# Fourier feature stage of a delta-rule attention and MLP kernel: cosine and sine sums kept apart for half of the outputs

## The chip, the cores and the metric

The kernel runs on one core of a Trainium2 chip. The metric is the device time of one execution in microseconds; lower is better. A core has five engines that run side by side, each with a queue of its own: PE (TensorE, matrix products; its weight loads are listed as PEld), DVE (VectorE), ACT (ScalarE), POOL (GpSimd) and SP, which here only issues DMAs. PE reads its operands from SBUF and writes to PSUM, from where DVE and ACT take the results.

## The reference

Three stages follow one another, on 4 batches of 768 positions and 384 features, all in fp32:

```python
# 1: delta-rule attention, 8 heads of 48; a state of 48x48 per head is carried over the positions
# 2: Fourier mixing and a feed-forward block
X = np.fft.fft(x, axis=1)
X = np.fft.fft(X, axis=2)
u = x + np.real(X)
un = (u - mean(u)) / sqrt(var(u) + 1e-6)
x2 = u + np.maximum(un @ w_ch1, 0.0) @ w_ch2
# 3: token mixing with cos and sin of x2 @ w_theta, then a second small feed-forward
```

The change lies in the second Fourier transform of stage 2, the one over the 384 features.

## The kernel before

Attention is worked off in chunks of 64 positions. When the 12 chunks of a batch are done, `fourier_inputs` forms sums and differences of that batch's rows and folds the features: because the cosine is even and the sine odd, feature d and feature 384-d are added for the cosine sums and subtracted for the sine sums, which leaves 384 folded rows instead of two times 384. `fourier_1` multiplies these by the position table `cs1` and leaves `G`, three chunks of 128 folded features by 385 position columns. Chunks 0, 1 and 2 of `G` hold the cosine rows 0 to 191, then 191 sine rows, and the cosine row 192 last.

Stage 2 works in 12 blocks, three per batch, of 256 positions each: position t and its mirror 768-t side by side (`u[:, 0]` and `u[:, 1]`). `prepare_1` multiplies `G` by the feature table `cs2` to get `pm`, 128 positions by 385 features. The mirrored positions need no product of their own: their feature e is feature 384-e of `pm`, read backwards. Only in the last block of a batch (`j == 2`) one row (position 384) is its own, and it has the small product `px`. Then come the adds to the residual `u`, the mean and the variance (`bn_stats`), and the normalised `un`. `prepare_2` transposes `un` on PE and splits it into a high and a low part. Twelve steps `f` follow per block: `ffn_up` gives `ph` (9 matmuls), ACT makes `hh` and DVE `hl` of it, and `ffn_down` adds six products into `pc`.

The order around the change is written out by hand: with `LEAD = (0, 4, 11)` the three parts of the next block's preparation (`prepare`, `prepare_1`, `prepare_2`) are issued at steps f = 0, 4 and 11 of the block before. So the adds of a block stand on DVE's queue between the `hl` evictions (L586) of the running block. Attention of the later batches is issued between the steps as filler. The compiler's planner then sets the final order on each engine from a simulated timeline. `pm`, `px`, `pg`, `ph` and `pt` share one PSUM pool of three buffers (tag `g`).

An fp32 matmul in the source shows as two matmul instructions in the trace, each streaming all its columns.

Of the kernel before, what the change touches and what calls it, by code (L numbers as in the profile page):

```python
# [10 lines left out]
F32 = mybir.dt.float32  # L11
# [8 lines left out]
DM = H * D  # L20
# [116 lines left out]
class Front:  # L137
# [60 lines left out]
    def mm(self, o, l, r):  # L198
        self.nc.tensor.matmul(o, l, r, start=True, stop=True, skip_group_check=True)  # L199

    def gram(self, w, c0=0, c1=2 * C):

# [183 lines left out]
    def fourier_inputs(self, b):  # L386

        nc = self.nc
        y = [self.y.pop((b, k)) for k in range(NT)]
        HD = DM // 2  # L390
        SQ = math.sqrt(3.0) / 2.0
        alone = b < FDVE

        def tt(o, a, c, op, dve=False):
            (nc.vector if dve or alone else nc.gpsimd).tensor_tensor(o, a, c, op)

        def new(nm):
# [12 lines left out]
        tt(y4, y4, y3, ALU.subtract)  # L410
        nc.scalar.activation(y4, y4, AF.Copy, scale=SQ)
        nc.vector.scalar_tensor_tensor(y3, y5, -0.5, t0, ALU.mult, ALU.add)
        tt(t0, t0, y5, ALU.add)
        tt(y5, y1, y2, ALU.subtract, True)
        tt(y1, y1, y2, ALU.add)
        nc.scalar.activation(y1, y1, AF.Copy, scale=-SQ)
        nc.vector.scalar_tensor_tensor(y2, y5, 0.5, y0, ALU.mult, ALU.add)
        tt(y0, y0, y5, ALU.subtract, True)

        def fold(o, d0, n, z, op, flip=False, dve=False):  # L420
            a = z[:, d0:d0 + n]
            r = z[:, DM - d0:DM - d0 - n:-1]
            if flip:
                a, r = r, a
            tt(o, a, r, op, dve)

        out = {}
        for r, zc, zn, p1, p2 in ((1, y2, y1, y5, t1), (2, y3, y4, y2, y1)):
            fold(p1[:, 0:HD], 0, HD, zc, ALU.add, dve=True)
            fold(p1[:, HD:DM - 1], 1, HD - 1, zn, ALU.subtract, dve=True)  # L430
            nc.scalar.activation(p1[:, DM - 1:DM], zc[:, HD:HD + 1], AF.Copy)
            fold(p2[:, 0:HD], 0, HD, zn, ALU.add)
            fold(p2[:, HD:DM - 1], 1, HD - 1, zc, ALU.subtract, flip=True)
            nc.scalar.activation(p2[:, DM - 1:DM], zn[:, HD:HD + 1], AF.Copy)
            out[f"p1{r}"], out[f"p2{r}"] = p1, p2
        for r, z, p in ((3, y0, y3), (0, t0, y4)):
            fold(p[:, 0:HD], 0, HD, z, ALU.add, dve=True)
            fold(p[:, HD:DM], 1, HD, z, ALU.subtract, flip=True)
            e = self.fz.tile([P, 32], F32, tag=f"e{r}", name=f"e{r}_{b}")
            nc.gpsimd.memset(e[:, 0:31], 0.0)  # L440
            nc.scalar.activation(e[:, 31:32], z[:, HD:HD + 1], AF.Copy)
            out[f"q{r}"], out[f"e{r}"] = p, e
        self.z[b] = out

    def fourier_1(self, b):
# [13 lines left out]
        for ch in range(KD):  # L459
# [19 lines left out]

    def residual(self, u, b, i):  # L480
# [43 lines left out]
    def prepare_1(self, b, j, u, un):  # L524
        nc, cs2, G = self.nc, self.cs2, self.G[b]
        HD = DM // 2
        k = f"{b}_{j}"
        pm = self.psg.tile([P, DM + 1], F32, tag="g", name=f"pm{k}")
        for ch in range(KD):
            nc.tensor.matmul(pm, G[:, ch, j * P:(j + 1) * P], cs2[:, ch, :], start=(ch == 0), stop=(ch == KD - 1))  # L530
        if j == 2:
            px = self.psg.tile([P, DM + 1], F32, tag="g", name=f"px{k}")
            for ch in range(KD):
                nc.tensor.matmul(px[64:65, 0:HD + 1], G[:, ch, DM:DM + 1], cs2[:, ch, 0:HD + 1], start=(ch == 0),
                                 stop=(ch == KD - 1))
        nc.vector.tensor_tensor(u[:, 0, :], u[:, 0, :], pm[:, 0:DM], ALU.add)
        v = u[:, 1, :]
        if j < 2:
            nc.vector.tensor_tensor(v, v, pm[:, DM:0:-1], ALU.add)
# [433 lines left out]
def constants():  # L973
# [55 lines left out]
```

## Time and profile before

| | |
|---|---|
| time, median of 3 runs (lowest, highest) | 1001.06 us (999.76, 1001.69) |
| span of the profiled execution (no other time is recorded for it) | 1217.0 us |
| mean granted clock of PE in it | 0.666 of full speed |
| PE busy (PEld) | 1126.0 us, 93% (957.3 us) |
| DVE, ACT, POOL busy | 682.7, 394.8, 387.5 us |

The profiled execution is 216 us longer than the median of the timed runs. All durations below are from it. "Busy" of PE counts the time in which any matmul is under way, and ends of matmuls are modelled.

### The profile page before, as it was taken

The numbers are of one execution on the slowest core, as the hardware profiler recorded it, in microseconds if no ns is written. First come the engines' busy times: TensorE is split into PE (matmuls) and PEld (weight loads), VectorE is DVE, ScalarE is ACT, GpSimd is POOL, SyncE is SP. The second block draws the span as 40 slices with busy tenths as digits, with TensorE's granted clock in tenths as the row PEclk, the third lists the DMA queues.
The fourth block names the chain that finished last, engine by engine and source line by source line (L and its number), as shares of the span: only waits on it lengthen the run. The fifth ranks groups of instructions, "written<-read, shape, count | busy, mean of one in ns | idle before, by whom it ended". The sixth has DMA issues, their size and how long they took to land.

```text
span 1217.0 us, 23437 instructions
## 1 busy us (share of the span) xinstructions
PE 1126.0 (93%) x9312; PEld 957.3 (79%) x9312; DVE 682.7 (56%) x1574; ACT 394.8 (32%) x982; POOL 387.5 (32%) x504
## 2 busy tenths in 40 slices
PE   5675664999999999999999999999999999999998
PEld 4564553778788888788888898888988888888887
DVE  5999999645666632576212464744579732450401
ACT  2243343423332343244352121212545411460300
POOL 5257764341131113024120242430235421350210
PEclk9995555666666666666666666666666666666666
DMA  6223431221030021012030021311132201110000
GB/s 190 70 87 94 121 110 50 79 72 60 29 110 21 28 86 59 27 40 68 27 106 14 26 78 40 91 40 32 47 104 65 85 14 35 38 40 20 20 13 26
DMA packets 42206, 71.87 MB, mean 59 GB/s; under 512 B 6833, under 2 KB 27057, under 8 KB 42097
## 3 DMA queue, kind: packets, MB, share of 16 engines
q1 hardware_dynamic: 41328, 68.02, 18.7%
q0 software_dynamic: 768, 2.36, 0.7%
q8 instruction: 73, 1.20, 0.4%
q14 instruction: 37, 0.30, 0.1%
HBM read 56.20 MB, written 14.16 MB: 58 GB/s over the span
## 4 chain that ended last, share of the span: by engine, by line
PE 83%; DVE 13%; issue 1%; DMA 1%; ACT 1%; POOL 0%; SPq 0%; ACTq 0%; DVEq 0%; POOLq 0%
PE pc L595 6%; PE ph L72 6%; PE ph L74 6%; PE ph L73 6%; PE pc L598 6%; PE pc L596 6%; PE ty L73 6%; PE ty L72 6%; PE ty L74 6%; PE sm L199 3%; PE pm L530 3%; DVE tmp L258 3%; DVE T L261 3%; PE py L199 2%; PE pg L457 2%; PE pu L199 2%
## 5 line engine op out<-in xcount | busy, mean ns | idle before, releaser
L586 DVE SCALAR_TENSOR_TENSOR hl<-ph,hh 128x256 fp32r<-128x256 f32 x144 | 60.1, 421 | 196.6 <-ACT hh L585 164.1
L72 PE MATMUL ph<-uh,w1h 128*128 128x256 f32 x432 | 151.9, 355 | 0.0
L74 PE MATMUL ph<-uh,w1l 128*128 128x256 f32 x432 | 148.5, 345 | 0.0
L73 PE MATMUL ph<-ul,w1h 128*128 128x256 f32 x432 | 148.2, 344 | 0.0
L595 PE MATMUL pc<-w2h,hh 128*128 128x384 f32 x288 | 127.6, 443 | 0.0
L585 ACT ACTIVATE hh<-ph 128x256 fp32r<-128x256 f32 x144 | 54.5, 383 | 208.6 <-PE ph L74 183.0
L596 PE MATMUL pc<-w2l,hh 128*128 128x384 f32 x288 | 121.4, 422 | 0.0
L199 PE MATMUL sm<-kt 48*64 48x128 f32 (+1 forms) x896 | 87.5, 354 | 30.7 <-DMA kt<-in_kq_dram 17.3
L73 PEld LDWEIGHTS ph<-ul,w1h 128*128 128x128 f32 x432 | 100.7, 233 | 6.6 <-issue 2.2
L72 PEld LDWEIGHTS ph<-uh,w1h 128*128 128x128 f32 x432 | 97.4, 226 | 8.3 <-issue 2.5
L74 PEld LDWEIGHTS ph<-uh,w1l 128*128 128x128 f32 x432 | 101.0, 234 | 2.3 <-issue 0.8
L199 PEld LDWEIGHTS sm<-kt 48*64 48x64 f32 x896 | 67.5, 186 | 43.7 <-ACT KQ L220 12.5
L598 PE MATMUL pc<-w2h,hl 128*128 128x384 f32 x288 | 98.2, 425 | 0.0
L261 DVE TENSOR_TENSOR T<-T,tmp 128x30 f32<-128x30 f32 (+9 forms) x180 | 73.1, 406 | 4.2
L258 DVE TENSOR_TENSOR tmp<-T 128x30 f32<-128x30 f32 (+9 forms) x180 | 72.9, 405 | 4.3
L284 POOL TENSOR_SCALAR_AFFINE_SELECT YQ<-KQ 64x512 f32<-64x512 f32 x48 | 33.1, 690 | 131.5 <-PE py L199 122.8
L199 PE MATMUL py<-X,YQ 112*64 112x48 f32 (+1 forms) x768 | 54.4, 259 | 22.3 <-ACT X L340 22.1
L595 PEld LDWEIGHTS pc<-w2h,hh 128*128 128x128 f32 x288 | 63.3, 220 | 8.4 <-issue 4.0
L596 PEld LDWEIGHTS pc<-w2l,hh 128*128 128x128 f32 x288 | 63.2, 220 | 7.2 <-issue 1.7
L199 PE MATMUL pu<-X,YU 128*64 128x48 f32 (+1 forms) x768 | 46.2, 262 | 23.6 <-ACT X L352 11.7
L199 PEld LDWEIGHTS py<-X,YQ 112*64 112x64 f32 (+1 forms) x768 | 45.3, 184 | 28.7 <-ACT X L340 23.9
L199 PEld LDWEIGHTS pu<-X,YU 128*64 128x64 f32 (+1 forms) x768 | 38.7, 181 | 33.9 <-ACT X L352 12.2
(282 smaller groups left out, 2524.6 us busy)
## 6 DMA issues: line engine op xcount, KB each, us to landing
kt<-in_kq_dram SPq DMA_DIRECT2D x96, 96.0 KB, 2.2
w_0raw<-in_w_dram SPq DMA_DIRECT2D x15, 384.0 KB, 3.4
YQ<-in_qt_dram SPq DMA_DIRECT2D x48, 96.0 KB, 2.4
Y<-in_kn_dram SPq DMA_DIRECT2D x48, 96.0 KB, 2.4
X<-in_v_dram SPq DMA_DIRECT2D x48, 96.0 KB, 2.5
ysc<-y SPq DMA_DIRECT2D x24, 192.0 KB, 2.1
x2scr<-u SPq DMA_DIRECT2D x12, 384.0 KB, 2.8
xt<-x2scr SPq DMA_DIRECT2D x24, 192.0 KB, 2.4
```

The lines of the kernel that those rows point to most:

```text
L72: nc.tensor.matmul(out, lh, rh, start=start, stop=False)
L73: nc.tensor.matmul(out, lh, rl, start=False, stop=False)
L74: nc.tensor.matmul(out, ll, rh, start=False, stop=stop)
L199: self.nc.tensor.matmul(o, l, r, start=True, stop=True, skip_group_check=True)
L258: nc.vector.tensor_tensor(pr, T[:, j + 1:, j:j + 1].to_broadcast([P, n, j]), T[:, j, 0:j].unsqueeze(1).to_broadcast([P, n, j]), ALU.mult)
L261: nc.vector.tensor_tensor(T[:, j + 1:, 0:j], T[:, j + 1:, 0:j], pr, ALU.add)
L530: nc.tensor.matmul(pm, G[:, ch, j * P:(j + 1) * P], cs2[:, ch, :], start=(ch == 0), stop=(ch == KD - 1))
L585: nc.scalar.activation(hh, ph, AF.Relu)
L586: self.up_end = nc.vector.scalar_tensor_tensor(hl, ph, 0.0, hh, ALU.max, ALU.subtract)
L595: nc.tensor.matmul(self.pc[i], hh[:, i * P:(i + 1) * P], wh, start=(f == 0), stop=False)
L596: nc.tensor.matmul(self.pc[i], hh[:, i * P:(i + 1) * P], wl, start=False, stop=False)
L598: nc.tensor.matmul(self.pc[i], hl[:, i * P:(i + 1) * P], wh, start=False, stop=(f == KF - 1))
```

## The change

`cs2` is cut from 385 output columns to 193, and kept apart for cosine and sine: four pieces of 128 rows by 193 columns instead of three of 128 by 385. The feature order is moved so that the 193 cosine rows come first and the 191 sine rows last. Chunk 0 of `G` is then all cosine, chunk 2 all sine, chunk 1 mixed. `pm` becomes two halves, cosine sums (`pm[:, 0]`) and sine sums (`pm[:, 1]`), 193 columns each. Feature e is their sum, feature 384-e their difference. ACT copies the cosine half to a new tile `c`, DVE forms the sum `lo` and the difference `hi` in `un`, and four adds of 193 or 191 columns bring them to the two halves of `u`, in place of two adds of 384 columns read from PSUM.

```diff
     def mm(self, o, l, r, start=True, stop=True):
...
-        self.cs2 = p.tile([P, KD, DM + 1], F32, name="cs2")
+        self.cs2 = p.tile([P, 4, DM // 2 + 1], F32, name="cs2")
...
+            fold(p1[:, HD + 1:DM], 1, HD - 1, zn, ALU.subtract, dve=True)
+            nc.scalar.activation(p1[:, HD:HD + 1], zc[:, HD:HD + 1], AF.Copy)
...
-            fold(p[:, HD:DM], 1, HD, z, ALU.subtract, flip=True)
+            nc.gpsimd.memset(p[:, HD:HD + 1], 0.0)
+            fold(p[:, HD + 1:DM], 1, HD - 1, z, ALU.subtract, flip=True)
             e = self.fz.tile([P, 32], F32, tag=f"e{r}", name=f"e{r}_{b}")
-            nc.gpsimd.memset(e[:, 0:31], 0.0)
-            nc.scalar.activation(e[:, 31:32], z[:, HD:HD + 1], AF.Copy)
+            nc.gpsimd.memset(e[:, 1:32], 0.0)
+            nc.scalar.activation(e[:, 0:1], z[:, HD:HD + 1], AF.Copy)
...
-                    mm(pg[64:128, cl], qq[:, 192:256], cs1[:, 1, cl], True, True)
+                    mm(pg[64:128, cl], qq[:, 192:256], cs1[:, 1, cl], True, False)
+                    mm(pg[64:96, cl], z[f"e{r}"], cs1[:, 0, cl], False, True)
                 else:
-                    mm(pg[:, cl], qq[:, lc], cs1[:, 1, cl], True, False)
-                    mm(pg[96:128, cl], z[f"e{r}"], cs1[:, 0, cl], False, True)
+                    mm(pg[:, cl], qq[:, lc], cs1[:, 1, cl], True, True)
...
     def prepare_1(self, b, j, u, un):
-        pm = self.psg.tile([P, DM + 1], F32, tag="g", name=f"pm{k}")
-        for ch in range(KD):
-            nc.tensor.matmul(pm, G[:, ch, j * P:(j + 1) * P], cs2[:, ch, :], start=(ch == 0), stop=(ch == KD - 1))
+        pm = self.psg.tile([P, 2, HW], F32, tag="g", name=f"pm{k}")
+        mm(pm, G[:, 1, js], cs2[:, 1:3, :], True, False)
+        mm(pm[:, 0, :], G[:, 0, js], cs2[:, 0, :], False, True)
+        mm(pm[:, 1, :], G[:, 2, js], cs2[:, 3, :], False, True)
         if j == 2:
-            px = self.psg.tile([P, DM + 1], F32, tag="g", name=f"px{k}")
-            for ch in range(KD):
-                nc.tensor.matmul(px[64:65, 0:HD + 1], G[:, ch, DM:DM + 1], cs2[:, ch, 0:HD + 1], start=(ch == 0),
-                                 stop=(ch == KD - 1))
-        nc.vector.tensor_tensor(u[:, 0, :], u[:, 0, :], pm[:, 0:DM], ALU.add)
-        v = u[:, 1, :]
-        if j < 2:
-            nc.vector.tensor_tensor(v, v, pm[:, DM:0:-1], ALU.add)
-        else:
-            nc.vector.tensor_tensor(v[0:64], v[0:64], pm[0:64, DM:0:-1], ALU.add)
-            m1 = un[:, 1, :]
-            nc.vector.tensor_copy(m1[64:128], pm[64:128, DM:0:-1])
-            nc.vector.tensor_copy(m1[64:65, 0:HD + 1], px[64:65, 0:HD + 1])
-            nc.vector.tensor_copy(m1[64:65, HD + 1:DM], px[64:65, HD - 1:0:-1])
-            nc.vector.tensor_tensor(v[64:128], v[64:128], m1[64:128], ALU.add)
+            px = self.psg.tile([P, HW], F32, tag="g", name=f"px{k}")
+            for ch in range(2):
+                mm(px[64:65, :], G[:, ch, DM:DM + 1], cs2[:, ch, :], ch == 0, ch == 1)
+        c = self.fz.tile([P, HW], F32, tag="c", name=f"c{k}")
+        nc.scalar.activation(c, pm[:, 0, :], AF.Copy)
+        lo, hi = un[:, 0, 0:HW], un[:, 1, 0:HW]
+        nc.vector.tensor_tensor(lo, c, pm[:, 1, :], ALU.add)
+        nc.vector.tensor_tensor(hi, c, pm[:, 1, :], ALU.subtract)
+
+        def add(v, p, q):
+            nc.vector.tensor_tensor(v[:, 0:HW], v[:, 0:HW], p, ALU.add)
+            nc.vector.tensor_tensor(v[:, HW:DM], v[:, HW:DM], q[:, HD - 1:0:-1], ALU.add)
+
+        add(u[:, 0, :], lo, hi)
+        if j == 2:
+            for x in (lo, hi):
+                nc.vector.tensor_copy(x[64:65], px[64:65, :])
+        add(u[:, 1, :], hi, lo)
```

Here `HD` is 192 and `HW` is 193. In `constants` the table `cs2` is built to match, with zeros where a row of chunk 1 belongs to the other sum.

## Rows read from the trace of the kernel before

**Rows 1.** Stretches: us, busy PE, PEld, DVE, ACT, POOL, granted clock, DMA share, GB/s.
```profile
0.00:50.00 50.00, 31.52 (x356) 27.33 (x358) 35.36 (x87) 13.15 (x24) 21.93 (x50) 1.00 0.54 150
...
200.00:210.00 10.00, 1.93 (x20) 1.68 (x21) 9.93 (x31) 3.98 (x13) 0.00 (x0) 0.50 0.00 1
...
224.00:229.00 5.00, 4.42 (x108) 4.02 (x104) 3.46 (x15) 3.68 (x11) 0.29 (x1) 0.65 0.01 3
...
215.00:840.00 625.00, 624.42 (x5792) 529.70 (x5792) 321.29 (x839) 198.77 (x541) 157.33 (x234) 0.65 0.18 55
840.00:1210.00 370.00, 368.30 (x1565) 311.47 (x1564) 164.43 (x308) 122.08 (x260) 108.60 (x111) 0.65 0.13 41
```

**Rows 2.** Chain of work that ended last, share of the span by engine.
```profile
PE 83%; DVE 13%; issue 1%; DMA 1%; ACT 1%; POOL 0%; SPq 0%; ACTq 0%; DVEq 0%; POOLq 0%
```

**Rows 3.** The same chain in order of time: start us, us, what.
```profile
309.99 2.94 PE pm L530 x6
312.93 1.50 PE px L534 x6
```

**Rows 4.** Instructions of the tile pm: count, duration ns minimum/median/maximum, first and last start.
```profile
L530 PE MATMUL pm<-cs,G x72: 624/696/738, 218.9 to 818.9; 128*128 128x385 f32 x72
L536 DVE TENSOR_TENSOR u<-u,pm x12: 549/554/555, 223.2 to 819.7; 128x384 f32<-128x384 f32 x12
L539 DVE TENSOR_TENSOR u<-u,pm x8: 547/548/556, 223.7 to 781.0; 128x384 f32<-128x384 f32 x8
L541 DVE TENSOR_TENSOR u<-u,pm x4: 536/538/539, 313.4 to 820.1; 64x384 f32<-64x384 f32 x4
L543 DVE COPY un<-pm x4: 560/561/561, 314.0 to 820.7; 64x384 f32<-64x384 f32 x4
```

**Rows 5.** Fourier matmuls pg in one run, 32 before the last row: start us, us.
```profile
734.23 1.39 PE L457 MATMUL pg<-cs,y 128*128 128x128 f32 x8
...
738.72 0.30 PE L457 MATMUL pg<-cs,e 128*32 128x64 f32 x2
```

**Rows 6.** Groups by line and shape, 215 to 830 us: busy us, mean ns, idle before.
```profile
L395 DVE TENSOR_TENSOR t<-y 128x192 f32<-128x192 f32 x1 | 0.4, 358 | 0.0
L395 DVE TENSOR_TENSOR y<-y 128x191 f32<-128x191 f32 x7 | 3.5, 497 | 0.0
L366 ACT ACTIVATE y<-py 128x192 f32<-128x192 f32 x18 | 5.9, 330 | 8.1 <-PE py L199 5.6 <-POOL y L395 2.2
L544 DVE COPY un<-px 1x193 f32<-1x193 f32 x4 | 1.4, 358 | 2.2 <-PE px L534 2.1
L546 DVE TENSOR_TENSOR u<-u,un 64x384 f32<-64x384 f32 x4 | 2.2, 555 | 0.1
L440 POOL MEMSET e<- 128x31 f32 x6 | 0.7, 124 | 3.8 <-PE pg L457 3.8
```

**Rows 7.** Timeline of the first block's preparation: start us, us.
```profile
223.25 0.56 DVE L536 TENSOR_TENSOR u<-u,pm 128x384 f32<-128x384 f32 x1 [1.39 <-PE pm L530]
...
230.07 0.69 PE L572 MATMUL pt<-ident,un 128*128 128x128 f32 x3
```

**Rows 8.** Timeline around two later preparations: adds, then hh and hl.
```profile
391.92 0.55 DVE L536 TENSOR_TENSOR u<-u,pm 128x384 f32<-128x384 f32 x1 [1.09 <-PE pm L530]
...
394.05 0.41 DVE L586 SCALAR_TENSOR_TENSOR hl<-ph,hh 128x256 fp32r<-128x256 f32 x1
...
453.52 0.55 DVE L536 TENSOR_TENSOR u<-u,pm 128x384 f32<-128x384 f32 x1 [6.36 <-PE pm L530]
...
457.38 0.38 ACT L585 ACTIVATE hh<-ph 128x256 fp32r<-128x256 f32 x1
457.80 0.42 DVE L586 SCALAR_TENSOR_TENSOR hl<-ph,hh 128x256 fp32r<-128x256 f32 x1
```

**Rows 9.** PE matmuls pu before 215 us, with the waits ahead of them.
```profile
L199 PE MATMUL pu<-X,YU 128*64 128x48 f32 x112 | 15.5, 306 | 23.4 <-ACT X L352 11.7 <-POOL X L299 6.2 <-POOL w2l L122 3.7
```

**Rows 10.** DMA issue of the table cs2: count, size, us to landing.
```profile
cs<-in_cs_dram SPq DMA_DIRECT2D x1, 577.5 KB, 5.7
```

More of the change, by code (lines that the diff above doesn't have):

```diff
@@ L196, in mw, with mm @@
         return self.psw.tile(shape, F32, tag="mw", name=name)
-    def mm(self, o, l, r):
-        self.nc.tensor.matmul(o, l, r, start=True, stop=True, skip_group_check=True)
+    def mm(self, o, l, r, start=True, stop=True):
+        self.nc.tensor.matmul(o, l, r, start=start, stop=stop, skip_group_check=True)
     def gram(self, w, c0=0, c1=2 * C):
@@ L429, in fourier_inputs @@
             fold(p1[:, 0:HD], 0, HD, zc, ALU.add, dve=True)
-            fold(p1[:, HD:DM - 1], 1, HD - 1, zn, ALU.subtract, dve=True)
-            nc.scalar.activation(p1[:, DM - 1:DM], zc[:, HD:HD + 1], AF.Copy)
+            fold(p1[:, HD + 1:DM], 1, HD - 1, zn, ALU.subtract, dve=True)
+            nc.scalar.activation(p1[:, HD:HD + 1], zc[:, HD:HD + 1], AF.Copy)
             fold(p2[:, 0:HD], 0, HD, zn, ALU.add)
-            fold(p2[:, HD:DM - 1], 1, HD - 1, zc, ALU.subtract, flip=True)
-            nc.scalar.activation(p2[:, DM - 1:DM], zn[:, HD:HD + 1], AF.Copy)
+            fold(p2[:, HD + 1:DM], 1, HD - 1, zc, ALU.subtract, flip=True)
+            nc.scalar.activation(p2[:, HD:HD + 1], zn[:, HD:HD + 1], AF.Copy)
             out[f"p1{r}"], out[f"p2{r}"] = p1, p2
@@ L526, in prepare_1 @@
         HD = DM // 2
+        HW = HD + 1
         k = f"{b}_{j}"
-        pm = self.psg.tile([P, DM + 1], F32, tag="g", name=f"pm{k}")
-        for ch in range(KD):
-            nc.tensor.matmul(pm, G[:, ch, j * P:(j + 1) * P], cs2[:, ch, :], start=(ch == 0), stop=(ch == KD - 1))
-        if j == 2:
-            px = self.psg.tile([P, DM + 1], F32, tag="g", name=f"px{k}")
-            for ch in range(KD):
-                nc.tensor.matmul(px[64:65, 0:HD + 1], G[:, ch, DM:DM + 1], cs2[:, ch, 0:HD + 1], start=(ch == 0),
-                                 stop=(ch == KD - 1))
@@ L536, in prepare_1 @@
[L536 to L546 removed]
+        js = slice(j * P, (j + 1) * P)
@@ new lines, in prepare_1 @@
+        pm = self.psg.tile([P, 2, HW], F32, tag="g", name=f"pm{k}")
+        mm = self.mm
+        mm(pm, G[:, 1, js], cs2[:, 1:3, :], True, False)
+        mm(pm[:, 0, :], G[:, 0, js], cs2[:, 0, :], False, True)
+        mm(pm[:, 1, :], G[:, 2, js], cs2[:, 3, :], False, True)
+        if j == 2:
+            px = self.psg.tile([P, HW], F32, tag="g", name=f"px{k}")
+            for ch in range(2):
+                mm(px[64:65, :], G[:, ch, DM:DM + 1], cs2[:, ch, :], ch == 0, ch == 1)
+        c = self.fz.tile([P, HW], F32, tag="c", name=f"c{k}")
@@ L977, in constants @@
     cs1 = np.stack([np.cos(a), np.sin(a)], axis=1)
-    d = np.concatenate([np.arange(DM // 2), np.arange(1, DM // 2), [DM // 2]])
-    even = np.concatenate([np.ones(DM // 2, bool), np.zeros(DM // 2 - 1, bool), [True]])
-    e = np.arange(DM + 1)
+    d = np.concatenate([np.arange(DM // 2 + 1), np.arange(1, DM // 2)])
+    cos = np.arange(DM) <= DM // 2
+    e = np.arange(DM // 2 + 1)
     a = 2.0 * np.pi * ((d[:, None] * e[None]) % DM) / DM
-    cs2 = np.where(even[:, None], np.cos(a), np.sin(a)).reshape(KD, P, DM + 1).transpose(1, 0, 2)
+    c, s = (x.reshape(KD, P, -1) for x in (np.where(cos[:, None], np.cos(a), 0.0), np.where(cos[:, None], 0.0, np.sin(a))))
+    cs2 = np.stack([c[0], c[1], s[1], s[2]], axis=1)
     return {"cs1": cs1.astype(np.float32), "cs2": cs2.astype(np.float32), "ident": np.eye(P, dtype=np.float32),
```

## The prediction, made before the changed kernel ran

> **What bounds the kernel now.** I read the busy time by stretch first. From 215 to 840 us PE is busy for 624.42 of 625 us and from 840 to 1210 us for 368.30 of 370, while DVE, the next, has 321 and 164 us [rows 1]. Before that it is another kernel: from 200 to 210 us DVE is busy for 9.93 of 10 us and PE for 1.93 [rows 1]. The chain of work that ended last says the same: PE holds 83% of the span, DVE 13% [rows 2]. So PE work taken out after 215 us shortens the end by its own length, unless a new wait replaces it; DVE and ACT work added there is free as long as no matmul waits for it. The first `pm` starts at 218.9 us and the last at 818.9 [rows 4], all inside the PE-bound stretch.
>
> The granted clock was 1.00, the 2.4 GHz level, in the first 50 us, 0.50, the 1.2 GHz level, from 200 to 210 us, and 0.65, between the two, in both long stretches [rows 1]. The timed runs need 1001.06 us where this execution spans 1217.0. If only PE's clock differs, the 992.7 busy us of the two long stretches must shrink to about 777, a clock near 0.83. I cannot see that; it is the main doubt about scaling.
>
> **The change part by part.**
>
> *Fewer columns through PE (the gain).* Before, a `pm` is six passes of 385 columns, back to back in 2.94 us, 0.490 us each [rows 3]; a 193-column pass of `px` takes 1.50/6 = 0.250 us [rows 3]. So time goes by columns, 1.27 and 1.30 ns each. Afterwards a `pm` is two passes of 386 columns and four of 193: 2 x 0.490 + 4 x 0.250 = 1.98 us, or 0.96 us less; for 12 blocks, 11.5 us. A `px` has four passes instead of six: 0.50 us less, four times, 2.0 us. Together 13.5 us. Would 193 columns be too few to hide the load of 128 weight columns? The Fourier matmuls `pg`, nearly all with loads of that size and with only 64 to 128 columns, come 32 in 738.72 - 734.23 = 4.49 us, 0.14 us apart [rows 5]. So a load fits well inside 0.250 us, and I charge nothing.
>
> *DVE and ACT in a block.* Before, the adds of a block with j < 2 are 554 + 548 = 1.10 us [rows 4]; with j = 2 they are 554 + 538 + 561 [rows 4], two copies of about 0.35 and one add of 0.555 [rows 6], 2.9 us. Afterwards DVE has six operations of 193 or 191 columns, and for j = 2 two copies of 0.358 [rows 6]. The nearest row for a six is an add of 192 columns at 0.358 us alone, 0.497 mean where POOL ran beside it [rows 6]. Two of the six read PSUM; 384 columns took 0.554 from PSUM [rows 4] and two adds of half that length at 0.358 make 0.72, so I take 0.358 for all. Then j < 2 costs 2.15 us, 1.05 more, in eight blocks: 8.4 us of DVE time; j = 2 stays at 2.9. Upper bound with the contended price on four of six: another 12 x 4 x 0.14 = 6.7 us. ACT gets 12 copies like the 128x192 one at 0.330 [rows 6], 4.0 us. DVE has 304 us free from 215 to 840, ACT 426 [rows 1]; PE covers this, and uncovered it would cost up to 19 us.
>
> *The longer way from the product to `un`.* The copy, then six operations, is 0.33 + 2.15 = 2.48 us against 1.10 before, 1.38 later. `prepare_2` is issued seven steps later, so in eleven blocks nobody waits for `un`. The first block has no step in progress: its add starts at 223.25 and the transposes at 230.07 [rows 7]. There PE has attention to do (busy for 4.42 of 5 us, 224 to 229 [rows 1]), and its `pm` comes 0.96 earlier. Bounds 0 and 1.38; I take +0.5.
>
> *Who stands behind the adds on DVE.* `hl`. In nine of the twelve blocks it comes over 3 us after the first add and waits for `hh`, as at 453.52 and 457.80; in three it comes within 2.2 us, as at 391.92 and 394.05 [rows 8]. A burst longer by 1.38 us fits the nine. In the three, `hl` and the product behind it can be late by up to 1.38 each, unless the planner puts `hl` first. Bounds 0 and 4.1; I take +1.5, nearer nothing since two thirds of that delay can be reordered away.
>
> *The rest.* Two more one-column memsets on POOL per batch, nearest row 0.124 us [rows 6], 1.0 us in all, on an engine that has 468 us free in the long stretch [rows 1]; in the DVE-bound start at most the first two, 0.25 us, and beside DVE's folds. The feature order moves the corner product from chunk 2 to chunk 1 of `G`: same count. `pm` now needs chunk 1 first, but always needed all three. The table load, 577.5 KB [rows 10], shrinks to 772/1155 of it; nobody waits for it. The buffers of tag `g` stay as long with the `pm` as before: copy and two operations, 1.05 us, against 1.10 for j < 2. All nothing.
>
> *Sum.* -13.5 + 0.5 + 1.5 = -11.5 us of 1217.0, to 1205.5, or -0.94%. On the median that is 1001.06 x 1205.5/1217.0 = 991.6 us.
>
> *A rule against it.* An add of 191 columns with both inputs in SBUF took 497 ns as a mean where the like one took 358 alone [rows 6]. The Trainium skill, page "SBUF — State Buffer", section "Who interferes with whom", says that a VectorE instruction with two SBUF inputs and a GpSimd instruction that reads SBUF exclude each other, the later one waiting for the whole of the earlier; the two durations agree with it. By that rule the 48 new adds would also hold up POOL; the price is below.
>
> **The rivals.**
>
> *A. The gain is partly swallowed (faster, less).* If the timed runs have PE at 1.00, the 13.5 us are only 13.5 x 0.65 = 8.8, and PE would need 992.7 x 0.65 = 645 of some 779 us, with waits for other engines in between. With half of it swallowed, 4.4 us are left: 996.7. For: the 216 us between profile and median. Against: a PE without gaps in every long stretch.
>
> *B. `hl` is late in every block (slower).* If the order puts `hl` behind the whole new chain everywhere and PE has nothing in between, each block loses 1.38 us: 12 x 1.38 = 16.6, less 13.5, plus 0.5, is +3.6: 1220.6, scaled 1004.0. It decides from 13.0/12 = 1.08 us exposed per block. For: the three tight blocks. Against: the nine with over 3 us.
>
> *C. POOL is held up (slower).* 48 adds of 0.358 are 17.2 us in which POOL may not read. If all of it reached PE through attention's inputs, +3.7 net of 13.5: 1220.7, 1004.1. PE did wait 6.2 us for POOL once, before 215 us [rows 9]; after 235 us the waits list none. That is the section named above, taken at its word.
>
> *D. It does nothing to the end.* Gain and late `hl` cancel, or PE's columns were never the limit in the timed runs: 1001.
>
> **How the numbers follow.** A difference under 0.2%, 2 us, cannot be told from none here. Forecast 0.62 (its own range 985 to 996), A 0.17 (995 to 999), D 0.08, B 0.10, C 0.03. So faster 0.79, same 0.08, slower 0.13. Low end: if PE ran at 0.50 throughout, the 13.5 us would be 13.5 x 0.65/0.50 = 17.6, 983.5; I put 984. High end: A whole and the first part of D, 1000.5, which leaves out B, C and the rest of D.
>
> **What would show it.** Right: `pm` x6 in about 2.0 us at clock 0.65, `px` x4 in 1.0; PE still busy for all but a few us after 215; DVE's busy time up by 8 to 15 us, ACT's by 4. Wrong if the six DVE operations take over 0.5 us each, if `hl` stands right behind them in more than a few blocks with PE idle before L598, or if the profile runs at another clock.

## The result: slower, by 0.6%

| | before | after |
|---|---|---|
| time, median (lowest, highest) | 1001.69 us, 5 runs (999.76, 1004.22) | 1008.32 us, 5 runs (1006.48, 1011.47) |
| ratio, 95% interval | | 1.0059 [1.0033, 1.0085] |
| span and mean clock of the profiled execution | 1217.0 us, 0.666 | 1004.8 us, 0.930 |

The forecast was 991.6 us. The two profiles in this table can't be laid side by side: before ran at another clock. The first experiment therefore profiled the kernel before once more, unchanged (1000.3 us, clock 0.946), and that trace is "before" from here on.

Page of the changed kernel, busy time and chain:

```profile
PE 875.2 (87%) x9304; PEld 809.5 (81%) x9304; DVE 697.6 (69%) x1614; ACT 394.1 (39%) x994; POOL 391.3 (39%) x512
...
PE 52%; DVE 34%; DMA 5%; issue 3%; ACT 2%; POOL 2%; SPq 0%; DVEq 0%; ACTq 0%; POOLq 0%
...
L607 PE MATMUL pc<-w2h,hl 128*128 128x384 f32 x288 | 76.2, 344 | 7.9 <-DVE hl L595 7.9
```

Page of the kernel before, profiled again:

```profile
PE 879.1 (88%) x9312; PEld 804.5 (80%) x9312; DVE 692.8 (69%) x1574; ACT 390.1 (39%) x982; POOL 390.3 (39%) x504
...
PE 55%; DVE 28%; DMA 5%; issue 4%; ACT 3%; POOL 2%; SPq 0%; ACTq 0%; POOLq 0%; DVEq 0%
...
L598 PE MATMUL pc<-w2h,hl 128*128 128x384 f32 x288 | 77.2, 345 | 2.5 <-DVE hl L586 2.4
```

The chain is the first thing to see. At the clock of the timed runs, even before the change PE holds 55% of it and DVE 28%, not the 83% and 13% of [rows 2]. PE's busy time fell by 3.9 us and DVE's rose by 4.8.

The changed operations themselves, in the views of tiles `pm` and `un` of the changed kernel (durations in ns minimum/median/maximum, first and last start), answer to [rows 4]. L542 is the copy, L544 and L545 are `lo` and `hi`, L548 and L549 the four adds into `u`:

```profile
L199 PE MATMUL pm<-cs,G x72: 324/327/592, 218.3 to 686.7; 128*128 128x193 f32 x48, 128*128 128x386 f32 x24
L542 ACT ACTIVATE c<-pm x12: 312/333/334, 220.7 to 687.0; 128x193 f32<-128x193 f32 x12
L544 DVE TENSOR_TENSOR un<-c,pm x12: 339/354/357, 221.4 to 687.4; 128x193 f32<-128x193 f32 x12
L545 DVE TENSOR_TENSOR un<-c,pm x12: 340/350/352, 221.7 to 687.7; 128x193 f32<-128x193 f32 x12
L548 DVE TENSOR_TENSOR u<-u,un x24: 342/353/648, 222.0 to 690.2; 128x193 f32<-128x193 f32 x24
L549 DVE TENSOR_TENSOR u<-u,un x24: 337/350/1165, 222.2 to 690.0; 128x191 f32<-128x191 f32 x24
```

One `pm` at full clock, PE's timeline of before and then of after, answers to [rows 3]:

```profile
587.68 2.11 PE L530 MATMUL pm<-cs,G 128*128 128x385 f32 x6
```

```profile
587.51 1.46 PE L199 MATMUL pm<-cs,G 128*128 128x386 f32 x6
```

0.65 us per `pm`, 7.8 us for twelve. The 0.65 us are four passes cut to half, 0.163 us each; every `px` loses two passes of that length, 1.3 us in four batches. So 9.1 us of PE work are gone, and the changed operations took what they were priced at. The loss is in waits, and the windows show in which stretches. Columns: stretch, us, busy PE, PEld, DVE, ACT, POOL, granted clock, DMA share, GB/s; before, then after:

```profile
220.00:510.00 290.00, 285.27 (x4000) 250.35 (x3999) 207.68 (x540) 131.07 (x361) 94.86 (x158) 1.00 0.25 73
510.00:745.00 235.00, 227.13 (x2019) 210.95 (x2018) 147.03 (x359) 86.61 (x231) 78.02 (x86) 1.00 0.22 65
745.00:1000.00 255.00, 233.07 (x1303) 225.99 (x1301) 137.68 (x251) 96.46 (x205) 98.02 (x97) 0.98 0.17 52
```

```profile
220.00:510.00 290.00, 279.66 (x3966) 250.46 (x3966) 211.63 (x556) 132.73 (x365) 93.43 (x160) 0.98 0.25 73
510.00:745.00 235.00, 226.40 (x2027) 213.19 (x2026) 152.08 (x386) 89.67 (x239) 79.73 (x88) 1.00 0.23 68
745.00:1000.00 255.00, 231.98 (x1287) 226.46 (x1287) 132.11 (x243) 95.35 (x203) 99.02 (x96) 0.96 0.15 47
```

PE's idle time in the three stretches is 4.7, 7.9 and 21.9 us before and 10.3, 8.6 and 23.0 us after (the change's last 4.8 us lie behind them). In the first stretch PE waits 5.6 us more than before: most of what the columns save there is waited away.

Beside it stands the view of tile `pc`, whose last add into `u` (`u<-u,pc`) ends stage 2. It starts at 743.7 us before and at 742.3 after: until there the change leads by 1.4 us. The spans, 1000.3 and 1004.8, say that it then loses 5.9 us, in the token mixing, of which no line was edited. So in these two executions there are two losses: most of the 9.1 us is not there when stage 2 ends, and the stage behind it is longer.

### The profile page after: what moved, and what is told of

It is laid out like the page before. It is cut to its first block, busy times and chain, and to the rows that moved or that the text cites. A ratio compares the mean times of both kernels' runs of the same rounds, so it can differ in the third digit from the quotient of the medians.

```text
span 1004.8 us, 23493 instructions
## 1 busy us (share of the span) xinstructions
PE 875.2 (87%) x9304; PEld 809.5 (81%) x9304; DVE 697.6 (69%) x1614; ACT 394.1 (39%) x994; POOL 391.3 (39%) x512
## 4 chain that ended last, share of the span: by engine, by line
PE 52%; DVE 34%; DMA 5%; issue 3%; ACT 2%; POOL 2%; SPq 0%; DVEq 0%; ACTq 0%; POOLq 0%
DVE tmp L258 5%; DVE T L261 5%; PE ty L74 4%; PE ty L72 4%; PE ty L73 4%; PE ph L74 4%; PE ph L72 4%; PE pc L604 4%; PE ph L73 4%; PE pc L607 3%; PE pc L605 3%; PE sm L199 2%; PE pg L458 2%; PE pu L199 2%; PE py L199 2%
## 5 line engine op out<-in xcount | busy, mean ns | idle before, releaser
L72 PE MATMUL ph<-uh,w1h 128*128 128x256 f32 x432 | 124.9, 292 | 2.1 <-DVE ul L583 2.1
L73 PE MATMUL ph<-ul,w1h 128*128 128x256 f32 x432 | 123.8, 287 | 2.3 <-DVE ul L583 2.3
L74 PE MATMUL ph<-uh,w1l 128*128 128x256 f32 x432 | 123.5, 287 | 0.0
L604 PE MATMUL pc<-w2h,hh 128*128 128x384 f32 x288 | 102.4, 355 | 2.3 <-ACT hh L594 2.3
L605 PE MATMUL pc<-w2l,hh 128*128 128x384 f32 x288 | 98.7, 343 | 0.0
L607 PE MATMUL pc<-w2h,hl 128*128 128x384 f32 x288 | 76.2, 344 | 7.9 <-DVE hl L595 7.9
L199 PE MATMUL py<-X,YQ 128*64 128x48 f32 (+1 forms) x768 | 48.9, 247 | 24.7 <-ACT X L340 24.5
L199 PEld LDWEIGHTS py<-X,YQ 128*64 128x64 f32 (+1 forms) x768 | 39.5, 160 | 29.9 <-ACT X L340 26.7
L199 PE MATMUL pu<-X,YU 128*64 128x48 f32 (+1 forms) x768 | 42.2, 253 | 19.8 <-ACT X L352 11.5
L607 PEld LDWEIGHTS pc<-w2h,hl 128*128 128x128 f32 x288 | 49.8, 190 | 10.1 <-DVE hl L595 9.6
L299 POOL TENSOR_TENSOR X<-X,nT 64x384 f32<-64x384 f32 x48 | 41.9, 874 | 41.1 <-DMA X<-in_v_dram 33.6
```

The source lines that it names most:

```text
L72: nc.tensor.matmul(out, lh, rh, start=start, stop=False)
L73: nc.tensor.matmul(out, lh, rl, start=False, stop=False)
L74: nc.tensor.matmul(out, ll, rh, start=False, stop=stop)
L199: self.nc.tensor.matmul(o, l, r, start=start, stop=stop, skip_group_check=True)
L299: nc.gpsimd.tensor_tensor(x[TK[par], par], x[TK[par], par], nT[TK[par], n].unsqueeze(2).to_broadcast([C, 8, D]), ALU.mult)
L604: nc.tensor.matmul(self.pc[i], hh[:, i * P:(i + 1) * P], wh, start=(f == 0), stop=False)
```

## What the later stage does differently

Between 794 and 799 us of the changed kernel PE stands for 5.15 us. ACT's timeline there (start us, us, in brackets the idle time before and what ended it):

```profile
791.37 0.53 ACT L906 ACTIVATE w2h<-xT 128x384 fp32r<-128x384 f32 x1
797.29 0.52 ACT L118 ACTIVATE w1h<-wti_384a 128x384 fp32r<-128x384 f32 x1 [5.39 <-DVE wti_384a L114]
797.72 0.56 ACT L855 ACTIVATE n<-pth,magic 128x384 f32<-128x384 f32 x1
798.19 0.48 ACT L845 ACTIVATE xT<-tt 128x384 f32<-128x384 f32 x1
798.56 0.49 ACT L846 ACTIVATE xh<-tt 128x384 fp32r<-128x384 f32 x1
```

And PE's:

```profile
793.61 0.34 PE L72 MATMUL tc<-w2h 128*128 128x384 f32 x1
799.10 0.69 PE L72 MATMUL pth<-wthh,xh 128*128 128x384 f32 x1 [5.15 <-ACT xh L846]
799.58 0.52 PE L73 MATMUL pth<-wthl,xh 128*128 128x384 f32 x1
```

And DVE's, the chain of the weight conversion for which ACT waits:

```profile
793.36 1.16 DVE L111 TENSOR_SCALAR wti_384raw<-wti_384raw 128x384 uint32<-128x384 uint32 x1
794.44 1.16 DVE L112 TENSOR_SCALAR wti_384a<-wti_384a 128x384 f32<-128x384 f32 x1
795.63 1.03 DVE L113 TENSOR_SCALAR wti_384a<-wti_384a 128x384 uint32<-128x384 uint32 x1
796.70 0.56 DVE L114 SCALAR_TENSOR_TENSOR wti_384a<-wti_384a,wti_384raw 128x384 uint32<-128x384 uint32 x1
```

Read from the bottom up: a conversion of a weight that PE does not need yet (`w1h` of the next `wti` block) was put on ACT's queue ahead of `xh`, which PE needs at once. ACT waits 5.39 us for DVE, `xh` waits behind it, PE waits for `xh`. Then the clock is low as well: the same 384 columns take 0.34 us before the gap and 0.69 and 0.52 behind it. The windows before, in and behind the gap have the granted clock in the column after POOL's, 1.00, 0.94 and then 0.50, the 1.2 GHz level:

```profile
788.00:794.00 6.00, 5.43 (x29) 4.84 (x29) 6.00 (x7) 1.84 (x4) 6.00 (x6) 1.00 0.38 126
794.00:798.00 4.00, 0.00 (x0) 0.00 (x0) 3.86 (x6) 0.71 (x2) 2.45 (x3) 0.94 0.36 97
798.00:801.00 3.00, 1.90 (x7) 1.81 (x8) 2.61 (x5) 1.70 (x5) 1.63 (x2) 0.50 0.01 2
```

So this stall cost more than its length. This order is the planner's choice. Theory O, stated now: the added operations move the planner's simulated time of the last preparation, it orders the token mixing otherwise, and that order costs the time. Rival W: the copy and the six operations cost it by their own work.

## The experiments

"Ratio" is against the kernel before on the same chip. "Stage 2" is the start of the last `u<-u,pc` of the profiled execution; its span minus that ("rest") is what the token mixing took, up to the last instruction. A profiled execution is one of the timed ones and can lie off their median: e6's is 3.8 us below it, e9's 4.2 us and e4's 2.2 us above, the change's 1.8 us below. So the last three columns tell where time goes, and the ratio tells how much.

| run | time us | ratio [95%] | stage 2 | span | rest |
|---|---|---|---|---|---|
| e1 before again | 1001.39 | 0.9997 [0.9984, 1.001] | 743.7 | 1000.3 | 256.6 |
| e2 feature order | 1003.14 | 1.0005 [0.9992, 1.0018] | 743.4 | 1000.5 | 257.1 |
| e3 products only | 998.2 | 0.9956 [0.9942, 0.997] | 740.5 | 996.6 | 256.1 |
| e4 evictions only | 1011.61 | 1.0087 [1.0072, 1.0103] | 745.4 | 1012.1 | 266.7 |
| e5 apart, all but last | 1001.09 | 0.9984 [0.9965, 1.0003] | 743.7 | 1000.9 | 257.2 |
| e6 apart, last only | 1002.94 | 1.0002 [0.9988, 1.0017] | 739.3 | 997.5 | 258.2 |
| e7 change, ahead | 1000.94 | 0.9985 [0.997, 1.0] | 741.5 | 999.4 | 257.9 |
| e8 before, ahead | 1009.72 | 1.0079 [1.0064, 1.0094] | 745.6 | 1006.1 | 260.5 |
| e9 products, first six | 1003.08 | 1.0013 [0.9996, 1.003] | 749.5 | 1005.6 | 256.1 |
| e10 products, last six | 994.96 | 0.9929 [0.9913, 0.9945] | 737.7 | 993.2 | 255.5 |
| e11 apart, first six | 1002.95 | 1.0006 [0.9991, 1.0021] | 743.6 | 999.3 | 255.7 |
| e12 apart, 6 to 10 | 999.53 | 0.9974 [0.9956, 0.9992] | 740.7 | 998.1 | 257.4 |
| e13 products, gather late | 993.26 | 0.9906 [0.9885, 0.9927] | 736.6 | 992.5 | 255.9 |
| e14 apart in last six | 997.35 | 0.9943 [0.993, 0.9956] | 739.9 | 995.6 | 255.7 |
| e15 evictions, ahead | 1000.55 | 0.9976 [0.9964, 0.9988] | 742.0 | 998.7 | 256.7 |
| e16 apart 6 to 11, ordered | 993.16 | 0.9907 [0.9889, 0.9925] | 735.3 | 990.9 | 255.6 |
| the change | 1008.32 | 1.0059 [1.0033, 1.0085] | 742.3 | 1004.8 | 262.5 |

**One part at a time.** e1: no edit.

> The kernel before, unchanged, for a profile at the clock at which the timed runs go: the one on record had PE at 0.65 and a span of 1217 us. Theory S (gaps): at 0.9 or more of the clock PE is no longer without gaps after 215 us, so some 60 to 130 us of that stretch are not PE's, and a column saved there is not always a microsecond saved. Theory P (PE-bound after all): PE is busy for over 98% of the stretch from 235 us to 20 us before the end here too. Both expect the median within 0.2% of the kernel before.

0.9997. It gave the trace at the timed runs' clock. From 235 to 980.3 us PE is busy for 716.4 of 745.3 us, 96%: there are gaps, so P falls, but after 215 us they come to 35 us and not to S's 60 to 130. e2: the feature order, its memsets and corner product, with 385 columns and the old adds.

```diff
-            fold(p1[:, HD:DM - 1], 1, HD - 1, zn, ALU.subtract, dve=True)
+            fold(p1[:, HD + 1:DM], 1, HD - 1, zn, ALU.subtract, dve=True)
...
-                    mm(pg[64:128, cl], qq[:, 192:256], cs1[:, 1, cl], True, True)
+                    mm(pg[64:128, cl], qq[:, 192:256], cs1[:, 1, cl], True, False)
+                    mm(pg[64:96, cl], z[f"e{r}"], cs1[:, 0, cl], False, True)
```

> Only the first half of the change: the order of the folded features (193 cosine rows first, then 191 sine rows, the corner product in chunk 1, the extra one-column memsets). Products of 385 columns and the adds are as before. No work of any length is added. Theory W (added work on DVE and ACT costs the time): 1.000, within 0.2%. Theory R (the planner's new order of unrelated work costs or gives it): a change as small as this already moves the time, by 0.3% or more in either direction.

1.0005: nothing, as W expected; R, which looked for 0.3% from so small an edit, missed. e3 adds the cut products, and leaves the old whole-width adds (the Fourier part of `u` is then not the reference's):

```diff
-        for ch in range(KD):
-            nc.tensor.matmul(pm, G[:, ch, j * P:(j + 1) * P], cs2[:, ch, :], start=(ch == 0), stop=(ch == KD - 1))
...
+        nc.tensor.matmul(pm, G[:, 1, js], cs2[:, 1, :], start=True, stop=False, **kw)
+        nc.tensor.matmul(pm[:, 0:HD + 1], G[:, 0, js], cs2[:, 0, 0:HD + 1], start=False, stop=True, **kw)
+        nc.tensor.matmul(pm[:, HD:DM + 1], G[:, 2, js], cs2[:, 2, HD:DM + 1], start=False, stop=True, **kw)
```

> On top of the new feature order only the products are shortened: 385 + 193 + 192 columns instead of 3 x 385, and two instead of three for px. The adds are those of before, so the output leaves out the separation of the two sums (features above 192 are not those of the reference); the work is what counts. Theory S: half or less of the saved 13.5 x 0.65/0.93 = 9.4 us arrives, ratio 0.995 to 1.000. Theory P: 0.990 to 0.992. Theory R: anything from 0.985 to 1.010, not the sum of its parts.

4.4 us gained by the ratio, half of the 9.1 us of PE work, in S's range and out of P's. e4 is the counterpart: the change's adds, with as many columns as before (the Fourier part is not the reference's).

```diff
-        mm(pm[:, 0, :], G[:, 0, js], cs2[:, 0, :], False, True)
-        mm(pm[:, 1, :], G[:, 2, js], cs2[:, 3, :], False, True)
+        mm(pm, G[:, 0, js], cs2[:, 0:2, :], False, False)
+        mm(pm, G[:, 2, js], cs2[:, 2:4, :], False, True)
...
```

> The changed kernel with the old amount of product columns: three products of 386 columns for pm and three of 193 for px, so that it sums cosine and sine chunks into both halves (not the transform of the reference). The copy to c and the six operations on DVE are those of the change. Theory W: slower than the changed kernel by what the columns are worth, 1.010 to 1.016 against before. Theory R: no closer than 0.5% to that.

1.0087, just under W's range (1.010 to 1.016), and R misses. By itself this would nearly fit W. But stage 2 ends at 745.4, 2.0 us behind e2, while the rest takes 9.6 us longer.

**Order or work.** The instructions of the token mixing stand in the order of before on every engine when the adds are left out of the last block alone, and nearly in that of the change when only the last block has them. In e5 eleven blocks have the change's adds, in e6 only the twelfth; the others add a flat row of `pm`:

```diff
+        if b * 3 + j < 11:
+            c = self.fz.tile([P, HW], F32, tag="c", name=f"c{k}")
...
+        else:
+            pf = pm.rearrange("p a b -> p (a b)")
+            nc.vector.tensor_tensor(u[:, 0, :], u[:, 0, :], pf[:, 0:DM], ALU.add)
...
```

> The changed kernel with the copy and the six operations in 11 of its 12 blocks; the last block (q = 11) adds the flat row of pm to u in the whole-width operations of before, on sums that are still kept apart, so that the Fourier part of the last block's tokens is left wrong. In the program that this gives, the token-mixing stage stands in the order of the kernel before on every engine. Theory O (the added operations of the last block shift the planner's simulated time, the planner then orders the token-mixing stage otherwise, and that order costs 6 to 10 us): 996 to 1000 us, 0.994 to 0.998 of before, last tc matmul 990 to 994 us after the start. Theory W (the copy and the adds themselves cost the time, in each block alike): 11/12 of the loss stays, 1006 to 1009 us.

> The mirror image: the copy and the six operations in the last block alone, whole-width adds on the sums kept apart in the other 11 (their Fourier part is left wrong). 37 added DVE and ACT operations become 4 or so; the token-mixing stage stands nearly in the order of the changed kernel. Theory O: 1003 to 1009 us (order's 6 to 10 us above the 998.2 of the products alone). Theory W: 1/12 of the loss, 998 to 1000 us.

e5: 1001.09 us, 0.9984 [0.9965, 1.0003]; e6: 1002.94, 1.0002 [0.9988, 1.0017]. Both lie between the two theories: by the ratios one block's adds cost 4.6 us over e3 and eleven blocks' adds 2.8. W's proportion, eleven to one, is refuted; O alone is not enough. The comparison of e5 with e3 is not a clean one: in the traces of e3 and e6 a row gather on POOL stands ahead of the folds of batch 2, in e5 behind them, and that place is worth 5.0 us (e3 to e13, below). Over e13 the adds of e5 cost 7.8 us.

e7 is the whole change, all operations in place; only the planner is told to place the last block's `prepare_1` earlier. With that its instructions from the last `u<-u,pc` on, compared in the traces by operation, tiles and shape, stand in before's order on every engine (those of the change differ in some 280 of 1308 places on PE and some 100 of 252 on DVE). Up to about 685 us its order is that of the change, one place on PE apart.

```diff
-            fr.prepare_1(b, j, *mid[q])
+            with tc.high_priority() if q == 11 else nullcontext():
+                fr.prepare_1(b, j, *mid[q])
```

> The whole change, nothing left out; the planner is told to give the instructions of prepare_1 of the last block a higher priority, and with that the token-mixing stage comes out in the order of the kernel before on POOL and SP and within a few places on DVE and ACT. Theory O: 996 to 1000 us, faster than both kernels, with up to the end of the feed-forward part what the changed kernel shows (its last block done near 743 us). Theory W: 1006 to 1010 us as the changed kernel, since every added operation is still there.

0.9985 against the change's 1.0059: the same instructions in another order are 7.4 us faster (0.74%). It stops 0.9 us short of O's range: the order is most of the loss, not all that keeps the change from gaining. e8 is the same edit in the kernel before.

> The kernel before, with the same higher priority for prepare_1 of its last block and no other edit: same instructions, same work, but the token-mixing stage falls into a third order that is on PE nearer to the changed kernel's than to its own. Theory O: the end moves by several us with no work added, most likely later, 1003 to 1010 us, and all of it after 740 us. Theory W: 1001 to 1003 us, no change.

1.0079: 8 us lost with no work added, in the profile 1.9 us before the end of stage 2 and 3.9 after it. So order alone can cost this much, and with e7 that shows O for the later stage. The price of one such order seems not to be fixed: e6, nearly in the change's order, took 258.2 us for the rest in its profile, the change 262.5. e15 repeats e7's edit on e4 (its Fourier part is that of e4).

> The changed kernel with full products (three of 386 columns for pm, three of 193 for px; G's cosine rows meet sine rows of the table, so the Fourier part is not the reference's) and prepare_1 of the last block at higher priority, so that the later stages stand in the order of before. It has the copies and adds of the change and none of its saving. Theory P (with full columns TensorE sets the pace of each block and the adds lie beside it): 1002 to 1005 us, 1.000 to 1.002. Theory W (the adds cost what is missing between e7 and e13, whatever TensorE does): 1009 to 1012 us, 1.006 to 1.009.

0.9976 against 1.0087: 11 us by the order. With columns full, the adds of all twelve blocks then show no cost: e2 has 1.0005. P holds, a little beyond its range on the fast side. But e15 is 2.9 us faster than e2 with more work in it, and its order in the earlier blocks isn't e2's; a cost of the adds could hide under what that order gives back. PE's waits after 745 us, e4 and then e15 (us in total, times, longest):

```profile
PE ty L72 <- ACT zrh L871: 8.6, 3, 5.3
PE pth L72 <- ACT xh L846: 5.2, 1, 5.2
PE ty L72 <- ACT w2h L871: 2.7, 1, 2.7
```

```profile
PE ty L72 <- ACT zrh L872: 5.7, 4, 2.3
PE tc L72 <- DVE xT L906: 3.1, 1, 3.1
PE pth L74 <- DVE xl L848: 2.5, 2, 1.7
```

The 5.3 and 5.2 us waits are those of the change; in before's order they are not there.

**Where half of the columns went.** e9 has the cut products in blocks 0 to 5, e10 in 6 to 11; old adds, so that the Fourier part of the blocks with cut products is not the reference's.

```diff
+        if b < 2:
             nc.tensor.matmul(pm, G[:, 1, js], cs2[:, 1, :], start=True, stop=False, **kw)
...
+        else:
+            for ch in range(KD):
+                nc.tensor.matmul(pm, G[:, ch, js], cs2[:, ch, :], start=(ch == 0), stop=(ch == KD - 1), **kw)
```

> Fewer columns in blocks 0 to 5 alone, the full 385 in blocks 6 to 11; whole-width adds as before in all blocks (blocks 0 to 5 get a Fourier part that is not the reference's). The later stages stand in the order of the kernel before. The twelve-block version measured 998.2 us, 4.4 under before. Theory M (what blocks 0 to 5 save is waited away at the feature stage of batch 2, whose input the attention chain delivers near 494 us whatever PE has spared): 1001 to 1003 us, at most 1 us gained. Theory H (a pass saves the same wherever it stands): half of 4.4, 999.5 to 1001 us.

> The mirror image: fewer columns in blocks 6 to 11 alone. Theory M: nearly the whole gain of the twelve-block version, 997.5 to 999.5 us (six blocks of 0.65 us and two px of 0.65 us are 5.2 us of PE time). Theory H: 999.5 to 1001 us.

e9: 1003.08 us, 1.0013 [0.9996, 1.003]; e10: 994.96, 0.9929 [0.9913, 0.9945]. e9 fits M, e10 gains more than M allows, and H falls. Half of the change of products is worth more than the whole, and the other half nothing. e10's 7.1 us are also more than the 4.6 us of PE work that six blocks save (6 x 0.65 and 2 x 0.33; the expectation counted a `px` double), so a part of them is not the columns. POOL's timeline in e9 shows the difference, at the start of batch 2:

```profile
484.99 1.01 POOL L395 TENSOR_TENSOR y<-y,y 128x385 f32<-128x385 f32 x1 [3.04 <-DVE y L395]
486.16 1.30 POOL L489 DMA_INDIRECT u<-ysc,rows  x1 [0.16 <-issue]
491.13 1.37 POOL L284 TENSOR_SCALAR_AFFINE_SELECT YQ<-KQ 64x512 f32<-64x512 f32 x2 [3.67 <-DMA u<-ysc,rows]
492.47 1.06 POOL L395 TENSOR_TENSOR t<-y 128x192 f32<-128x192 f32 x2
```

The row gather of block 6 was placed ahead of the folds (`t<-y`); the next instruction on POOL waits 3.67 us until it has landed (3.44 us in e3), and the folds, the feature stage and `pm` of block 6 come later. In e10 the gather follows the folds, all but one. e13 ties it there, behind the fold `y<-t`, with cut products in all twelve blocks.

```diff
+        self.fold_end = f_end[-1]
...
-            mid[q] = fr.prepare(b, j)
+            with tc.issue_after(fr.fold_end.ins) if q == 6 else nullcontext():
+                mid[q] = fr.prepare(b, j)
```

> Fewer columns in all 12 blocks, whole-width adds as before (Fourier part not the reference's), later stages in the order of the kernel before, and the residual loads of block 6 (with GpSimd's row gather) ordered behind the last fold of batch 2. Without that order the same kernel measured 998.2 us, 0.9956 of before; fewer columns in the last six blocks alone 995.0, 0.9929. Theory G (the gather ahead of the folds costs the saving of blocks 0 to 5): 993 to 995.5 us, 0.990 to 0.993. Theory M (the attention chain sets when the feature stage of batch 2 starts, wherever the gather stands): 997 to 999 us, 0.995 to 0.997.

993.3 us, 0.9906, against 0.9956 for e3. G, and M falls. POOL's timeline:

```profile
488.10 1.28 POOL L396 TENSOR_TENSOR t<-y 128x192 f32<-128x192 f32 x2
...
491.12 0.70 POOL L396 TENSOR_TENSOR y<-t 128x191 f32<-128x191 f32 x1 [0.63 <-DVE y L396]
...
492.99 1.00 POOL L493 DMA_INDIRECT u<-ysc,rows  x1 [0.27 <-POOL X L299]
494.05 0.53 POOL L396 TENSOR_TENSOR y<-y 128x191 f32<-128x191 f32 x1
```

In the traces the orders of e3 and e13 are the same on DVE and SP and differ on the other engines in a few places, nearly all between 480 and 550 us, so the place of the gather is the cause of these 5.0 us. With it restored the cut products gain 9.4 us (0.0094 of 1003; 7.3 to 11.5 by the interval), as much as the 9.1 us of PE work. Other places of e13's order still differ from before's, so that the two agree may in part be luck.

**Which adds.** e11 and e12 have cut products everywhere and the change's adds in blocks 0 to 5 and 6 to 10 alone (the other blocks' Fourier part is not the reference's); the edit is e5's with `b < 2` and `6 <= b * 3 + j < 11`.

> Fewer columns in all blocks; the copy and the six adds and subtractions in blocks 0 to 5 alone, whole-width adds on the sums kept apart in the others (their Fourier part is left wrong); later stages in the order of the kernel before. The same with the adds in blocks 0 to 10 measured 1001.1 us, with them in none 998.2. Theory D (the adds cost where VectorE is fully busy with the attention solves, up to about 490 us, and nothing after): 1000.5 to 1002 us, the whole 2.9. Theory E (each block's adds cost the same): 999.3 to 1000 us.

> The mirror image: the copy and the six operations in blocks 6 to 10 alone, fewer columns in all. Theory D: 997.5 to 999 us, as with no adds at all. Theory E: 999.3 to 1000 us.

e11: 1002.95 us, 1.0006 [0.9991, 1.0021]; e12: 999.53, 0.9974 [0.9956, 0.9992]. e11 lies above the ranges of both theories, e12 in E's. Neither tells much: e12 has e9's early gather again (2.89 us of POOL's time), e11 has not, and the two costs over e3, 5.0 and 1.8 us, do not add up to e5's 2.8. Over e13, whose gather is late as theirs, e11 costs 10.0 us and e5 7.8. e16 repeats e12 with block 11 as well and with both orders tied, as in e13 and e7.

> Fewer columns in all blocks; the copy and six operations in blocks 6 to 11, whole-width adds on the sums kept apart in blocks 0 to 5 (their Fourier part is left wrong); the gather of block 6 behind the folds and prepare_1 of the last block at higher priority. Between e13 (993.3, 0.9906, adds in none) and e7 (1000.9, 0.9985, adds in all). Theory D (the adds cost where VectorE has no free time, in blocks 0 to 5, and 1 to 2 us in the six others): 994 to 996 us, 0.991 to 0.994. Theory E (each block's adds cost the same): 996 to 998 us, 0.994 to 0.996.

0.9907, e13's 0.9906, a little beyond D's range on the fast side: in blocks 6 to 11 the adds cost nothing that can be measured. And e14 leaves nothing out: whole products in blocks 0 to 5, the change in 6 to 11, the second table loaded over the first.

```diff
+        if b < FULL:
+            self.whole(b, j, u, un)
+        else:
+            self.apart(b, j, u, un)
...
+                nc.sync.dma_start(fr.cs2.rearrange("p a b -> p (a b)")[:, 0:4 * (DM // 2 + 1)], io["cs3"].rearrange("p a b -> p (a b)"))
...
+        lo, hi, c = (uf[:, i * HW:(i + 1) * HW] for i in range(3))
```

> Nothing left out: blocks 0 and 1 of the batches (blocks 0 to 5) with whole products and adds as before, blocks 6 to 11 with the sums apart and the copy and six operations of the change; the second table is loaded over the first after block 5's product, and the copy c lies in a free part of un. The later stages stand in the order of the kernel before. Theory O with M or G (order kept in both places, columns saved where they count, adds where VectorE is not full): 995 to 998 us, 0.993 to 0.997, faster than both kernels. Theory W (the adds cost in each block): 1000 to 1003 us.

997.35 us, 0.9943 [0.993, 0.9956]: in O's range, and faster than both kernels.

## Why the prediction was wrong

**The step that failed** is the first one: "PE work taken out after 215 us shortens the end by its own length, unless a new wait replaces it", with the waits judged from a trace in which PE ran at two thirds of its clock [rows 1]. That the profile might run at another clock is one of the prediction's own signs of being wrong, and it did. At the clock of the timed runs PE is idle 22 of 255 us in the last stretch of before, shown above, and new waits did replace the work: in the change PE waits 5.6 us more between 220 and 510 us, and the token mixing is 5.9 us longer.

**Columns: the mechanism held, the size was that of rival A.** 13.5 us at clock 0.65 was the forecast, 11.1 on the median. Rival A's 8.8 at full clock is close to the 9.1 read and to e13's 9.4. With cut products alone half of the gain went into a wait on POOL (e3 to e13) that has nothing to do with `pm`. In the change itself the gather stands behind the folds (at 494.57 us), so this wait is no part of its loss.

**DVE and ACT work: rightly priced; covered where it could be seen.** The six operations took 0.35 us each as a median and the copy 0.33, as charged; back to back the six start 0.27 us apart (from 221.44 us on). DVE's busy time rose by 4.8 us and ACT's by 4.0 (8.4 and 4.0 forecast; 8 to 15 for DVE was a sign of being right). e16 shows no cost of the adds in blocks 6 to 11. In blocks 0 to 5, beside fewer columns, it is the open term below.

**The rest at nothing: right.** e2, with the feature order, the memsets and the corner product, is 1.0005. The first block's +0.5 was not tested by itself.

**`hl`: under-sized.** PE waited 7.9 us for `hl` in stage 2 against 2.4 before (the two pages above): +5.5 instead of +1.5, beyond the upper bound of 4.1. So a part of rival B's mechanism came, not its 16.6 us; and the two longest of these waits (2.08 and 2.37 us) stand behind other work than the six operations, as shown for e7 below.

**What no step held: the order of everything else.** The prediction let the planner only put `hl` first. It costed the edit inside the order of before. In fact the order moved in places that the diff does not touch: in the change in the token mixing, which costs 7.4 us (e7), against the 9.5 us that the forecast took off the median; with cut products alone on POOL at block 6. Rivals B and C had the right sign, neither this mechanism. The ratios split the 5.9 us of the result like this: -9.4 (cut products with the gather late, e13), 0.1 (the adds in blocks 6 to 11, e16), +7.8 (the adds in blocks 0 to 5 with the order that they bring, e16 to e7), +7.4 (the later order, e7 to the change). These are steps of one chain of runs, so that they add up is no check.

**What stays open** is the third term, 7.8 us. It isn't the adds' work on DVE alone: e15 has the same DVE instructions as e7 and more PE work, but another order, and is through block 5 earlier. Tile `pc` between 530 and 545 us, e15 and then e7 (first and last start of the two adds):

```profile
L610 DVE TENSOR_TENSOR u<-u,pc x2: 544/546/548, 536.2 to 536.7; 128x384 f32<-128x384 f32 x2
```

```profile
L610 DVE TENSOR_TENSOR u<-u,pc x2: 544/550/555, 539.7 to 540.3; 128x384 f32<-128x384 f32 x2
```

Between 220 and 510 us PE waits in e7 for `hl`, in e16 for `hh` and hardly for `hl` (0.1 us). The longest waits of both, e7 and then e16 (us in total, times, longest):

```profile
PE pc L607 <- DVE hl L595: 5.1, 4, 2.4
PE pc L604 <- ACT hh L594: 2.0, 2, 1.3
```

```profile
PE pc L622 <- ACT hh L612: 3.6, 1, 3.6
PE ph L72 <- DVE ul L601: 1.8, 1, 1.8
```

Two of e7's waits for `hl` make 4.2 of the 5.1 us: 1.76 us at 316.01 and 2.39 at 481.17. The second, on PE's timeline:

```profile
478.44 0.34 PE L605 MATMUL pc<-w2l,hh 128*128 128x384 f32 x1
481.17 0.62 PE L607 MATMUL pc<-w2h,hl 128*128 128x384 f32 x2 [2.39 <-DVE hl L595]
```

On DVE this `hl` stood behind the two transposes of an attention solve, folds and copies, the other behind copies of a solve, a `bn_stats` and a fold, and none of the six operations stood directly ahead of either. That fits the order of blocks 0 to 5 as the cause. But no run gave the whole change before's order in these blocks, so it stays open how much of the 7.8 us is the order and how much the adds beside a PE that comes to `hl` earlier.

## What to carry over

Where a planner orders the engines' queues, an edit is two edits: its work, and a new order for code it never touches; here an order alone was worth 5 to 11 us (e3 to e13, e7, e8, e15), the work of the edit at most 9. Before explaining a small loss, find the stretch where it arises, and if that isn't the edited one, give the edit the old order (a priority, a tie behind one instruction) and time it again. Take a profile at the clock of the timed runs before pricing work as covered: this kernel had PE for 83% of its chain at two thirds of the clock, and for 55% at the clock of the timed runs, where it also waits for DVE, ACT and POOL.

## What the hardware showed unexpectedly

The kernel before ran once at a mean clock of 0.666 (0.65 for 995 us [rows 1]) and, profiled again, at 0.946, 216.7 us shorter. All its variants ran at 0.925 to 0.981.

The DVE conversions L111 and L112 took 1.16 us each while POOL ran instructions back to back from 786.77 to 796.45 us, in the changed kernel; in e7 the same lines took 0.35 each at 798.53 and 798.80, when POOL had nothing from 798.2 to 800.66. The Trainium skill, page "SBUF — State Buffer", section "Who interferes with whom", says that a `tensor_scalar` can enter a mode that holds the port pair shared with GpSimd, so that the later of the two waits for the whole of the other; these rows agree. Rival C looked for that in the new adds, where it was rare: the four with both inputs in SBUF took 0.35 us as a median, the longest 0.65 and 1.17 (L548 and L549 above).
